# An mLSTM cell feeding a top-1 expert layer: two tiles per expert taken from a count frozen at chunk 18 and run during the routing of the last tiles

## The chip, the cores and the metric

One Trainium2 chip, one of its cores. The metric is the device time of one execution in microseconds; lower is better. Engines are named as in the profile: PE is TensorE (PEld its weight loads), DVE VectorE, ACT ScalarE, POOL GpSimd, SP SyncE.

## What is computed

`q, k, v, o_gate` are (4, 8, 768, 40) in float32, the gates (4, 8, 768). The first part is a recurrence over 768 steps for each batch and head, the second a layer of eight experts on the 3072 rows that come out of it:

```python
for t in range(S):
    m_new = np.maximum(f_gate[:, :, t] + m, i_gate[:, :, t])
    f_stab, i_stab = np.exp(f_gate[:, :, t] + m - m_new), np.exp(i_gate[:, :, t] - m_new)
    C = f_stab * C + i_stab * einsum('bhd,bhe->bhde', vt, kt)
    n = f_stab * n + i_stab * kt
    y[:, :, t] = sigmoid(o_gate[:, :, t]) * (C @ qt) / max(|n . qt|, 1)
x = y.transpose(0, 2, 1, 3).reshape(3072, 320)
logits = x @ w_gate                      # (3072, 8)
expert_idx = logits.argmax(1); gate_w = softmax(logits)[expert_idx]
out = gate_w * (relu(x @ w1[expert_idx]) @ w2[expert_idx])   # 320 -> 1024 -> 320
```

(Shapes are shortened.) With the inputs used, the experts get 508, 638, 184, 320, 431, 317, 284 and 390 rows.

## The kernel before

**The recurrence** is done in 24 chunks of 128 rows (six per batch), in the parallel form: scores of the chunk's rows against each other, plus a state `C` carried from chunk to chunk. The order on every engine is written out by hand: iteration `s` of the loop (from -3) computes the scores of chunk s+1, transposes q and k of s+2, updates the state of s, finishes chunk s (`attend`, `rows`), and routes older chunks. SP issues the loads (L229), six chunks ahead, k, q, v and the output gate each by itself. `rows` (L319 to L325) gives the row tile `x_sb`; `xtrans` (L332) transposes it for the gate logits (L354).

**The routing** goes by pairs of tiles (`teams`), the last two tiles one by one. `choose` takes the best expert of each row, `rank` counts by matmuls with a triangular and a ones matrix how many rows of each expert came before, `place` turns that into a slot. Each expert owns a region of 3200 rows of the DRAM tensor `x_sorted`; `keep_rows` scales a tile by its gate value into `x_all`, and `send` (L447) scatters it from POOL by an indirect DMA. `clear` (L453) zeroes the first 384 rows of each region; ACT issues these eight DMAs during iterations 0 to 3. POOL also issues all loads of the expert weights, since they are cast from float32 to bfloat16 on the way (L167 for w1, in three parts, L171 for w2); experts 0 and 1 are loaded at iterations 17 to 21. `warm` (L434) runs matmuls whose result is not used ("junk"), up to thirty after the last send.

**The experts.** After the last send has landed, SP reads three tiles per expert (384 rows, L593) back into `x_all`. Then groups run in order: experts 0 to 7 with three tiles each, and then six "extra" tiles of experts with more than 384 rows (five are needed here; if more than six were, a loop at the end would run them). A group is: transposes of the row tiles (`turn`, L624), layer 1 (L633: 24 matmuls of 384 columns, results `hp`, relu on DVE and ACT by turns into `h_sb`), the transposes of the next group, layer 2 (L646: eight matmuls per tile, result `zp`), a copy `zo` on ACT (L651) and a scatter to the output from POOL (L652). Weights of experts 2 to 4 are issued after the last send, those of expert 5+i at group i. `extras` works out which tiles are left over, `blank` writes a zero tile after each expert's last row, `collect` fetches an extra tile, `fetch` copies the weights of its expert (`wx`).

Of the kernel before, what the change touches and what calls it, by code (L numbers as in the profile page):

```python
# [19 lines left out]
def kernel(  # L20
# [44 lines left out]
    XU = 6  # L65
    XW = 4
# [46 lines left out]
    for name, shape, pattern, base, mult in (  # L113
        ("first_w", [128, E], [[-1, E]], E, 0),
        ("cum0", [128, E], [[NS // 128, E]], 0, 0),
        ("pos", [128, E, NJ], [[NS, E], [1, NJ]], 0, NJ),
        ("thr", [128, E, NX], [[NS, E], [128, NX]], CAP, 0),
        ("eb", [128, E], [[NS, E]], CAP, 0),
        ("kx", [128, NX], [[1, NX]], 0, 0),
        ("rowx", [128, NX], [[128, NX]], 0, 1),  # L120
    ):
        iotas[name] = (
            consts.tile(shape, I32, name=name + "_i"), consts.tile(shape, F32, name=name), pattern, base, mult,
        )
    first_w, cum0, pos, thr, eb, kx, rowx = (iotas[n][1] for n in iotas)
# [4 lines left out]
    tick = consts.tile([1, 1], F32)  # L130

    def late_consts(i):
# [12 lines left out]
        lo, hi_ = ((0, 2), (2, 4), (4, 7))[i - 2] if 2 <= i <= 4 else (0, 0)  # L145
# [15 lines left out]
    tot = rte.tile([128, E], F32)  # L161

# [20 lines left out]

    def router():
        nc.vector.tensor_scalar_mul(wg_sb[:], wg_sb[:], -1.0)
# [6 lines left out]
    with tc.tile_pool(name="ring", bufs=1) as ring_pool, \  # L192
# [6 lines left out]
        kp, qp, v1 = (  # L199
            [ring_pool.tile([128, H, w], F32, name=f"{n}{i}") for i in range(NV)]  # L200
            for n, w in (("kp", DP), ("qp", DP), ("v1_", D1))
        )
# [58 lines left out]
        def scores(s):  # L261
# [3 lines left out]
            sB = ps1.tile([128, PR, 128], F32, name="sB")  # L265
            for j in range(PR):
# [70 lines left out]
        teams = [(t, t + 1) for t in range(0, NT - 2, 2)] + [(NT - 2,), (NT - 1,)]  # L337
# [8 lines left out]

        def logits(P, host):

            r = rt[P] = {"t": teams[P], "n": len(teams[P])}
            lg, fresh = spare(host)  # L350
            r["lg"] = lg[:, : r["n"] * E]
# [78 lines left out]
        def warm(n):  # L430
            j = ps1.tile([128, 512], F32, name="junk", tag="tk")
            kb = st[NT - 1]["kb"]
            for _ in range(n):
                nc.tensor.matmul(  # L434
                    j[:], lhsT=kb[:, 0, :], rhs=kb[:].rearrange("p j t -> p (j t)"), start=True, stop=True,
                )
# [7 lines left out]
        def send(t):  # L444
            if t >= NT - 7:
                nc.gpsimd.memset(tick[:], 0.0)
            apart(nc.gpsimd.indirect_dma_start(  # L447
                out=xs[:, :], out_offset=bass.IndirectOffsetOnAxis(ap=slots[:, t : t + 1], axis=0),
                in_=x_all[:, t, :], in_offset=None,
            ), "rows_in")  # L450

        def clear(e):
            nc.scalar.dma_start(xs[e * NS : e * NS + CAP, :].rearrange("(p j) d -> p (j d)", j=NJ), zrow[:])  # L453
# [17 lines left out]
        for s in range(-3, NT):  # L471
# [10 lines left out]
            if 0 <= s < E // 2:  # L482
                nc.vector.memset(w1_all[:64, DB - 1, 2 * s : 2 * s + 2, :], 0.0)
                clear(2 * s)
                clear(2 * s + 1)
            if not odd and P >= 0:
                gate(P)
            do(states, s)
            do(load, s + 6 if s >= -1 else -1)
            if not odd and P >= 0:  # L490
                rank(P, s - 1)
            if last:
                warm(2)
                attend(s)
            do(xtrans, s - 1)
            do(ogate, s + 2)
            if not last:
                do(attend, s)
            if s == NT - 2:
                warm(3)  # L500
            if not odd and P >= 0:
                place(P)
            do(keep_rows, s - 4)
            do(rows, s)
            if odd and s >= 3:
# [5 lines left out]
            if 17 <= s < 20:  # L511
                weights_in(0, 2, (s - 17,))
            if 20 <= s < 22:
                weights_out(s - 20, 1)
        P = len(teams) - 3
        send(NT - 5)
        xtrans(NT - 1)
        gate(P)
        rank(P, NT - 1)
        place(P)  # L520
        logits(P + 1, NT)
        choose(P + 1)
        count(P + 1)
        logits(P + 2, NT + 1)
# [3 lines left out]
        gate(P + 1)  # L528
        warm(3)
        rank(P + 1, NT, E)  # L530
        place(P + 1)
        keep_rows(NT - 2)
        send(NT - 2)
        choose(P + 2)
        gate(P + 2)
        warm(3)
        rank(P + 2, NT + 1, E)
        place(P + 2)
        keep_rows(NT - 1)
        send(NT - 1)  # L540
        nc.vector.tensor_copy(tot[:], rt[P + 2]["tot"])
        warm(30)

    xg = [x_all[:, e * NJ : (e + 1) * NJ, :] for e in range(E)]
    sm_pool = ctx.enter_context(tc.tile_pool(name="moe_sm", bufs=1))
    s_idx = sm_pool.tile([128, E, NJ], I32)
    inv = sm_pool.tile([128, E, NJ], F32)
# [39 lines left out]
    mps_pool = ctx.enter_context(tc.tile_pool(name="moe_ps", bufs=3, space=PSUM))  # L587

    def ids_of(t):
        return t[:, :, Dm:].bitcast(I32).rearrange("p j o -> p (j o)")  # L590

    def receive(e):
        nc.sync.dma_start(  # L593
            xg[e].rearrange("p j d -> p (j d)"), xs[e * NS : e * NS + CAP, :].rearrange("(p j) d -> p (j d)", j=NJ),
        )

    def targets(e):
        nc.vector.scalar_tensor_tensor(
            s_idx[:, e, :], in0=inv[:, e, :], scalar=float(N), in1=ids_of(xg[e]), op0=ALU.mult, op1=ALU.add,
        )  # L600
# [11 lines left out]
    def aim(g):  # L612
# [4 lines left out]
        g["si"] = lambda j: t[:, 0:1]  # L617

    def turn(g):
        g["xT"] = wk_pool.tile([128, DB, NJ * 128], BF16, name="xgT")  # L620
        for j in range(g["n"]):
            tp = mps_pool.tile([128, DB, 128], BF16, name="tp", bufs=3)
            for db in range(DB):
                nc.tensor.transpose(tp[:, db, :], g["xg"][:, j, wch[db] : wch[db] + 128], ident_b[:])  # L624
            nc.vector.tensor_copy(g["xT"][:, :, j * 128 : (j + 1) * 128], tp[:])

    def layer1(g):
        cols = g["n"] * 128
        g["h"] = wk_pool.tile([128, FB, NJ * 128], BF16, name="h_sb")
        for fb in range(FB):  # L630
            hp = mps_pool.tile([128, NJ * 128], F32, name="hp")
            for db in range(DB):
                nc.tensor.matmul(  # L633
                    hp[:, :cols], lhsT=g["w"][0][:, db, fb * 128 : (fb + 1) * 128],
                    rhs=g["xT"][:, db, :cols], start=(db == 0), stop=(db == DB - 1),
                )
            if fb % 2 == 0:
                nc.vector.tensor_relu(g["h"][:, fb, :cols], hp[:, :cols])  # L638
            else:
                nc.scalar.activation(g["h"][:, fb, :cols], hp[:, :cols], AF.Relu)  # L640

    def layer2(g):
        for j in range(g["n"]):
            zp = mps_pool.tile([128, Dm], F32, name="zp", bufs=2)
            for fb in range(FB):
                nc.tensor.matmul(  # L646
                    zp[:], lhsT=g["h"][:, fb, j * 128 : (j + 1) * 128], rhs=g["w"][1][:, fb, :],
                    start=(fb == 0), stop=(fb == FB - 1),
                )
            zo = wk_pool.tile([128, Dm], F32, name="zo", bufs=8)  # L650
            nc.scalar.copy(zo[:], zp[:])  # L651
            ins = nc.gpsimd.indirect_dma_start(  # L652
                out=out[:, :], out_offset=bass.IndirectOffsetOnAxis(ap=g["si"](j), axis=0),
# [96 lines left out]
```

## Time and profile before

| what | us |
|---|---|
| runs (three) | 231.73, 233.25, 237.22; median 233.25 |
| profiled execution, its own time | 236.67 |
| its span (first to last instruction) | 234.8 |
| PE, PEld, DVE, ACT, POOL busy in it | 209.9, 169.5, 133.5, 122.7, 124.8 |
| last chunk's L319 | starts at 123.59 |
| first layer 1 of an expert | starts at 142.94 |
| last scatter to the output | issued at 229.63 |

The page divides the span into 40 slices of 5.87 us and gives the busy tenths of each engine, the clock that TensorE was granted, and the DMA engines' share; views of the trace give the same for any stretch, the single instructions in order of time, and what each waited for. Idle time that a row had before it stands in brackets with what ended it. TensorE's ends are modelled, so a full digit says that it had work, not that it ran at its peak; how many matmuls a stretch holds, and the granted clock, say more.

### The profile page before, as it was taken

The page shows a single profiled execution, that of the slowest core. Times are in us where ns is not written, and L with a number is a line of the kernel's source. Part 1 is how long each engine was busy: PE and PEld are TensorE (multiplying, and loading weights), DVE is VectorE, ACT ScalarE, POOL GpSimd, SP SyncE. Part 2 cuts the span into 40 slices and gives each one's busy share as a digit, 9 for nine tenths or more (in the row PEclk, how much of TensorE's full clock was granted, in tenths as well). Part 3 has the DMA queues.
Part 4 walks back from the last instruction along what each step waited for, and adds up shares of the span by engine and source line. Part 5 has one row for each costly group of instructions (what it writes and reads, how often), then busy time and mean ns, then how long its engine had stood idle before and what let it go on. Part 6 is the DMA issues. An engine that isn't in the chain of part 4 may idle for free.

```text
span 234.8 us, 5415 instructions
## 1 busy us (share of the span) xinstructions
PE 209.9 (89%) x1870; PEld 169.5 (72%) x1870; DVE 133.5 (57%) x446; ACT 122.7 (52%) x301; POOL 124.8 (53%) x195
## 2 busy tenths in 40 slices
PE   1389799999999999999998977999959999999990
PEld 1279699999999999999987334756627666668770
DVE  7657754445788888888867203873322453334540
ACT  2557445538688988898836101434223444444440
POOL 5045544343766686689986870433454765433331
PEclk9999955556999999999979597999979999999996
DMA  8999999984979999999697399999999999937900
GB/s 136 191 183 233 210 222 224 191 147 84 171 127 189 177 181 190 200 187 174 120 152 128 68 192 291 239 212 218 235 236 255 227 386 379 375 139 274 355 20 0
DMA packets 121723, 46.45 MB, mean 198 GB/s; under 512 B 102425, under 2 KB 114844, under 8 KB 121696
## 3 DMA queue, kind: packets, MB, share of 16 engines
q1 hardware_dynamic: 106272, 27.52, 54.8%
q0 software_dynamic: 13808, 16.40, 35.5%
q10 hardware_dynamic: 1616, 2.19, 2.6%
q8 instruction: 15, 0.25, 0.4%
q14 instruction: 12, 0.10, 0.1%
HBM read 39.38 MB, written 9.53 MB: 208 GB/s over the span
## 4 chain that ended last, share of the span: by engine, by line
PE 63%; DMA 14%; SPq 7%; DVE 6%; ACT 4%; issue 3%; POOL 2%; ACTq 0%; DVEq 0%; POOLq 0%
PE hp L633 14%; PE zp L646 9%; PE hp L354 7%; PE hp L287 7%; SPq L229 7%; DMA out_dram<-zo,s_idx 6%; PE dC L295 5%; PE tk L254 4%; PE xt L332 4%; PE tq L254 3%; PE sA L267 3%; DMA x_all<-x_sorted 3%; DMA qp<-in_q_dram 2%; DMA o_sb<-in_o_gate_dram 2%; PE hp L307 2%
## 5 line engine op out<-in xcount | busy, mean ns | idle before, releaser
L638 DVE TENSOR_SCALAR h_sb<-hp 128x384 bf16<-128x384 f32 (+1 forms) x56 | 24.6, 443 | 45.9 <-PE hp L633 29.6
L640 ACT ACTIVATE h_sb<-hp 128x384 bf16<-128x384 f32 (+1 forms) x56 | 22.2, 399 | 34.0 <-PE hp L633 33.5
L633 PE MATMUL hp<-xgT,w_all 128*128 128x384 bf16 x192 | 36.0, 345 | 3.8 <-ACT h_sb L640 2.5
L652 POOL DMA_INDIRECT out_dram<-zo,s_idx x24 | 24.0, 999 | 21.8 <-ACT zo L651 9.5
L633 PEld LDWEIGHTS <-w_all 128*128 128x128 bf16 x192 | 19.5, 102 | 18.3 <-issue 7.7
L325 POOL TENSOR_TENSOR x_sb<-x_sb,den 128x320 f32<-128x320 f32 x23 | 16.6, 721 | 27.4 <-DVE den L323 27.3
L646 PEld LDWEIGHTS <-h_sb 128*128 128x128 bf16 x240 | 22.9, 98 | 8.0
L651 ACT COPY zo<-zp 128x320 f32<-128x320 f32 x30 | 12.8, 425 | 30.1 <-PE zp L646 23.0
L447 POOL DMA_INDIRECT x_sorted<-x_all,slots x24 | 25.0, 1040 | 5.8 <-issue 3.5
L646 PE MATMUL zp<-w_all,h_sb 128*128 128x320 bf16 x192 | 27.4, 299 | 0.0
L334 ACT COPY xT<-xt 128x384 f32<-128x384 f32 x24 | 11.6, 482 | 22.7 <-PE xt L332 13.7
L287 PE MATMUL hp<-C_sb,qT 104*128 104x82 f32 x160 | 23.0, 292 | 0.0
L287 PEld LDWEIGHTS hp<-C_sb,qT 104*128 104x128 f32 x160 | 22.2, 214 | 0.5 <-DVE den L321 0.3
L254 PE MATMUL tk<-ident,kp 128*104 128x128 f32 x96 | 18.5, 324 | 4.2 <-DMA kp<-in_k_dram 4.2
L295 PE MATMUL dC<-vA,kp 128*104 128x82 f32 x160 | 21.0, 284 | 0.0
L354 PE MATMUL hp<-wg_sb,xT 128*128 128x8 f32 x144 | 20.3, 273 | 0.0
L295 PEld LDWEIGHTS dC<-vA,kp 128*104 128x104 f32 x160 | 19.6, 200 | 0.0
L354 PEld LDWEIGHTS hp<-wg_sb,xT 128*128 128x128 f32 x144 | 19.5, 215 | 0.1
L275 POOL TENSOR_SCALAR_AFFINE_SELECT dB<-dB 128x512 bf16<-128x512 bf16 x24 | 16.0, 667 | 5.2 <-ACT dB L274 5.0
L274 ACT CAST dB<-sB 128x512 bf16<-128x512 f32 x24 | 14.0, 582 | 8.4 <-PE sB L268 8.3
L242 POOL CAST vAb<-vA 128x328 bf16<-128x328 f32 x24 | 11.0, 459 | 13.4 <-DVE vA L240 12.5
L254 PE MATMUL tq<-ident,qp 128*104 128x128 f32 x96 | 17.5, 314 | 0.5 <-DMA qp<-in_q_dram 0.5
(130 smaller groups left out, 419.5 us busy)
## 6 DMA issues: line engine op xcount, KB each, us to landing
w_all<-in_moe_w_dram POOLq DMA_DIRECT2D x8, 640.0 KB, 13.6
wx<-w_all SPq DMA_DIRECT2D x6, 768.0 KB, 6.1
kp<-in_k_dram SPq DMA_DIRECT2D x24, 160.0 KB, 3.7
qp<-in_q_dram SPq DMA_DIRECT2D x24, 160.0 KB, 3.8
v<-in_v_dram SPq DMA_DIRECT2D x24, 160.0 KB, 4.0
o_sb<-in_o_gate_dram SPq DMA_DIRECT2D x24, 160.0 KB, 4.5
wx<-w_all SPq DMA_DIRECT2D x6, 640.0 KB, 9.6
w_all<-in_moe_w_dram POOLq DMA_DIRECT2D x13, 256.0 KB, 13.9
```

The source lines that it names most:

```text
L229: nc.sync.dma_start(d[n][:, :, :D], src[b, :, c * 128 : (c + 1) * 128, :].rearrange("h p d -> p h d"))
L254: nc.tensor.transpose(tp[:, j, :], two(d[n], j), ident[:])
L287: nc.tensor.matmul(hp[:, 2 * j * D1 : (2 * j + 2) * D1], lhsT=d["qT"][:, j, :], rhs=st["C"][:, j].rearrange("p h d -> p (h d)"), start=(j ...
L295: nc.tensor.matmul(st["dC"][:, j], lhsT=two(d["k"], j), rhs=d["vA"][:, 2 * j : 2 * j + 2, :], start=(c == 0 and j == 0), stop=True, skip_g ...
L325: eng.tensor_tensor(x3d, x3d, den[:].unsqueeze(2).to_broadcast([128, H, D]), op=ALU.mult)
L354: nc.tensor.matmul(lg[:, i * E : (i + 1) * E], lhsT=st[t]["xT"][:, db * 128 : (db + 1) * 128], rhs=wg_sb[:, db, :], start=(fresh and i == ...
L447: apart(nc.gpsimd.indirect_dma_start(out=xs[:, :], out_offset=bass.IndirectOffsetOnAxis(ap=slots[:, t : t + 1], axis=0), in_=x_all[:, t, : ...
L633: nc.tensor.matmul(hp[:, :cols], lhsT=g["w"][0][:, db, fb * 128 : (fb + 1) * 128], rhs=g["xT"][:, db, :cols], start=(db == 0), stop=(db == ...
L638: nc.vector.tensor_relu(g["h"][:, fb, :cols], hp[:, :cols])
L640: nc.scalar.activation(g["h"][:, fb, :cols], hp[:, :cols], AF.Relu)
L646: nc.tensor.matmul(zp[:], lhsT=g["h"][:, fb, j * 128 : (j + 1) * 128], rhs=g["w"][1][:, fb, :], start=(fb == 0), stop=(fb == FB - 1),)
L652: ins = nc.gpsimd.indirect_dma_start(out=out[:, :], out_offset=bass.IndirectOffsetOnAxis(ap=g["si"](j), axis=0), in_=zo[:], in_offset=None ...
```

## The change

- The routing's teams are pairs throughout (the last two tiles go together).
- At team 8 (tiles 16 and 17, the first 18 of 24) the counts are frozen by `even_out`: they are read out, and each expert that has fewer than 256 rows gets its count raised to 256, so that later rows lie behind row 256. The first two tiles of every expert (256 rows) are then final.
- `receive` reads them in the last iteration of the loop, waiting only for the sends up to tile 17. The first two experts' first two tiles run between the routing steps of tiles 20 to 23, in the buffers of the recurrence. There are no junk matmuls in the tail any more.
- Afterwards the groups are (2, first two), (0, third tile), (3, first two), (1, third tile), and so on, and then the six extra tiles. Layer 1 fills a whole PSUM bank (512 columns) before each relu.
- Weights: experts 0 and 1 in iterations 20 to 23, expert 2 in the tail, expert e+1 at group (e, first two): w1 before its layer 1, w2 after it.
- `clear` is issued from SP, in iterations -1 to 2; the memsets of the padding of w1 are halved and spread over iterations 0 to 7.
- Before the scores of chunks 1 to 7 stand three matmuls with 512 columns whose result is overwritten, before those of chunks 21 to 23 two.

```diff
@@ receive, turn and layer1 (moved ahead of the loop, tiles by part) @@
+    def receive(e, part):
+        r0, j = e * NS + part * NE * 128, (NE, NJ - NE)[part]
+        ins = nc.sync.dma_start(
+            xg[e][part].rearrange("p j d -> p (j d)"), xs[r0 : r0 + j * 128, :].rearrange("(p j) d -> p (j d)", j=j),
+        )
+        if part == 0:
+            tc.add_to_no_dep_group("early", getattr(ins, "ins", ins))
...
+    def layer1(g, u):
+        n = g["n"]
+        per = 4 // n
...
+        hp = spot("hp", [128, per, n * 128], F32)
+        for i in range(per):
+            fb = u * per + i
+            for db in range(DB):
+                nc.tensor.matmul(
+                    hp[:, i, :], lhsT=g["w"][0][:, db, fb * 128 : (fb + 1) * 128], rhs=g["xT"][:, db, :],
+                    start=(i == 0 and db == 0), stop=(db == DB - 1), skip_group_check=True,
+                )
@@ scores @@
+            for _ in range(3 if 1 <= s < 8 else 2 if s > NT - 4 else 0):
+                nc.tensor.matmul(
+                    sA[:].rearrange("p j t -> p (j t)"), lhsT=ident_b[:],
+                    rhs=st[s - 1]["dA"][:].rearrange("p j t -> p (j t)"), start=True, stop=True,
+                )
@@ even_out (new), send, clear @@
+            nc.tensor.matmul(c, lhsT=ones_b[:], rhs=row, start=False, stop=True, skip_group_check=True)
+            nc.vector.tensor_copy(cnt[:], c)
+            nc.vector.tensor_tensor(short[:], cnt[:].unsqueeze(2).to_broadcast([128, E, NE]), fill[:], op=ALU.is_lt)
+            for j in range(NE):
+                with nc.allow_low_precision("whole numbers up to 256"):
+                    nc.vector.tensor_tensor(row, row, short[:, :, j], op=ALU.add)
+            nc.vector.tensor_tensor(
+                inv[:, :, :NE], posA[:], cnt[:].unsqueeze(2).to_broadcast([128, E, NE]), op=ALU.is_ge,
+            )
...
+            if t > 2 * PE_ + 1:
+                tc.declare_no_dep(getattr(ins, "ins", ins), group="early", reason="later rows lie behind the early tiles")
...
-            nc.scalar.dma_start(xs[e * NS : e * NS + CAP, :].rearrange("(p j) d -> p (j d)", j=NJ), zrow[:])
+            nc.sync.dma_start(xs[e * NS : e * NS + CAP, :].rearrange("(p j) d -> p (j d)", j=NJ), zrow[:])
@@ the loop @@
-                clear(2 * s)
-                clear(2 * s + 1)
...
+            if -1 <= s < 3:
+                clear(2 * s + 2)
+                clear(2 * s + 3)
...
+            if last:
+                for e in range(E):
+                    receive(e, 0)
...
+            if s == 20:
+                weights_in(0, 1, (0, 1))
+            if s == 21:
+                weights_in(0, 1, (2,))
+            if s == 22:
+                weights_out(0, 1)
+            if last:
+                weights_in(1, 1, range(DB))
@@ the tail @@
+        weights_out(1, 1)
         send(NT - 5)
+        gate(P0)
+        rank(P0, NT - 1)
+        place(P0)
...
+        targets(0, 0)
+        turn(first)
         for t in (NT - 4, NT - 3):
             keep_rows(t)
             send(t)
+        for u in range(4):
+            layer1(first, u)
+        xtrans(NT - 1)
+        targets(1, 0)
+        turn(second)
+        layer2(first, 0)
+        logits(P0 + 1, NT)
+        choose(P0 + 1)
+        gate(P0 + 1)
+        layer2(first, 1)
+        layer1(second, 0)
+        rank(P0 + 1, NT, 2 * E)
+        place(P0 + 1)
+        nc.vector.tensor_copy(tot[:], rt[P0 + 1]["tot"])
+        weights_in(2, 1, range(DB))
+        layer1(second, 1)
+        for t in (NT - 2, NT - 1):
+            keep_rows(t)
+            send(t)
+        for u in range(2, 4):
+            layer1(second, u)
+        weights_out(2, 1)
+        layer2(second, 0)
+        layer2(second, 1)
@@ the groups @@
+    for e in range(E):
+        receive(e, 1)
+    order = [(2, 0), (0, 1)]
+    for e in range(3, E):
+        order += [(e, 0), (e - 2, 1)]
+    order += [(E - 2, 1), (E - 1, 1)]
...
+        if g.get("k") == 0 and nw < E:
+            weights_in(nw, 1, range(DB))
+        for u in range(FB * g["n"] // 4):
+            layer1(g, u)
+        if g.get("k") == 0 and nw < E:
+            weights_out(nw, 1)
         if i + 1 < len(groups):
+            ready(groups[i + 1])
+        for j in range(g["n"]):
+            layer2(g, j)
```

`ready` is `targets` (output rows of a group's slots, one DVE operation) and `turn`; `nw` is the group's expert plus one.

## The prediction

> **What bounds the kernel now.** I read the page's slices first, then the granted clock in stretches, then the rows where a stretch changes. The profiled execution took 236.67 us (span 234.8); the median of the runs is 233.25, so 3.4 us less. I work out differences on the profile and apply them to the median.
>
> The slices on the page: busy tenths of TensorE, its granted clock, the DMA engines.
>
> ```profile
> span 234.8 us, 5415 instructions
> PE   1389799999999999999998977999959999999990
> PEclk9999955556999999999979597999979999999996
> DMA  8999999984979999999697399999999999937900
> ```
>
> TensorE is busy nearly everywhere, but at half clock in slices 6 to 9 and again around slices 21 and 22; one digit low (slice 28) is a stop in the expert stage. DMA is nearly full all along. The clock by stretches (columns: length, busy time and count of PE, PEld, DVE, ACT, POOL, granted clock, DMA share, GB/s):
>
> ```profile
> 26.00:30.00 4.00, 2.24 (x29) 1.98 (x29) 3.04 (x8) 2.78 (x6) 2.44 (x7) 0.96 1.06 245
> 30.00:56.00 26.00, 26.00 (x179) 24.94 (x179) 11.87 (x44) 13.86 (x35) 9.59 (x21) 0.50 0.90 174
> 57.00:117.00 60.00, 59.87 (x722) 57.48 (x722) 49.82 (x173) 51.81 (x131) 45.08 (x63) 1.00 0.97 172
> 118.00:122.00 4.00, 4.00 (x31) 3.30 (x31) 3.29 (x13) 1.57 (x7) 3.17 (x5) 0.57 1.19 170
> ```
>
> So the recurrence (chunks 0 to 23) is bound by TensorE, first at 0.50 and then at 1.00. By the row L319, one per chunk, chunk 2 ends at 27.84, chunk 7 at 59.91, chunk 8 at 65.00, chunk 14 at 88.76: 6.41 us per chunk cold, 3.96 warm. The timeline before the drop:
>
> ```profile
> 24.71 1.63 ACTq L453 DMA_DIRECT2D x_sorted<-zrow  x2
> 27.01 0.52 PE L332 MATMUL xt<-ident,x_sb 128*128 128x128 f32 x3 [0.75 <-ACT xT L334]
> 28.73 0.21 PE L267 MATMUL sA<-qb,kb 40*128 40x128 bf16 x1 [1.01 <-ACT qb L256]
> ```
>
> ScalarE spends 1.63 us issuing two clears (L453), its copies come late, TensorE stands 0.75 and 1.01 us for them, and at 30 the clock halves. The routing tail, in the timeline:
>
> ```profile
> 130.31 9.18 PE L434 MATMUL junk<-kb 104*128 104x512 bf16 x30
> ...
> 131.91 0.96 POOL L447 DMA_INDIRECT x_sorted<-x_all,slots  x1 [0.21 <-issue]
> ...
> 135.50 4.00 SPq L593 DMA_DIRECT2D x_all<-x_sorted  x8
> ...
> 141.42 0.68 PE L624 MATMUL tp<-ident_b,x_all 128*128 128x128 bf16 x9 [1.94 <-DMA x_all<-x_sorted]
> ```
>
> I set t = 0 at the last L319 (123.59). Until t+17.8 TensorE does nothing for the experts: the last send goes at t+8.3, lands at 135.2, its rows come back 5.87 us later. From t+17.8 to the span's end are 93.4 us. An expert of three tiles has a period of 7.66 (187.85, 195.51, 203.17), an extra tile 3.07 (210.50, 213.56); eight and six make 79.7. The last zp ends 5.9 before the span's end. So 7.8 are cold matmuls and the stop at 170 to 172.7.
>
> **What the Trainium skill says.** "TensorE: Matmul & The Clock Gate", Part 1: the array runs at half clock until about 3.4 us of activity, and falls back after an idle window. The trace has both clocks, but the drop at 30 follows idle gaps of only 1 us and stays for 26 us of busy matmuls, so being busy is not enough here. The same page, Part 2, has matmuls in program order: a transpose that waits holds all behind it. "DMA: Bandwidth & Descriptors", "Issuing engines are not separate DMA queues": another issuer saves only issue time; the 1.63 us of ScalarE above are such time. Its "Anatomy of one DMA" gives 2.0 us plus bytes/436e3 for GpSimd's transfers: as an estimate 5.0 us for a w1 (1.31 MB of f32). The trace shows more; see below.
>
> **The change, part by part.**
>
> *Front.* Eight clears move from ACT to SP: 8 x about 0.8 us off ScalarE, the two gaps (1.8 us of TensorE) gone. SP gets 8 issues between the loads. Its loads run ahead: chunk 8's o load is issued at 36.36, and warm chunk 6 would need that chunk's k and q at about 39, so I cost the move at nothing with thin cover; if it is gone, loads are the bound at 4.9 us per chunk (issues at 21.79, 26.63, 31.55, 36.36). Three matmuls of 128x512 before the scores of chunks 1 to 7: warm 0.215 each (the junk pair of L434 took 0.43), so 21 x 0.215 = 4.5 us, all on TensorE's path; cold 0.41 each (three in 1.24). If they hold the clock, chunks 3 to 7 cost 5 x 3.96 = 19.8 instead of 32.1: -12.3. Net -7.8. The eight half-size memsets replace four, hidden by idle DVE.
>
> *End of the loop.* 118 to 122 at 0.57: 4 x 0.43 = 1.7 us to win with the matmuls before the last three scores (6 x 0.215 = 1.3); five junk matmuls (1.24 + 0.43 = 1.7) go. -2.1. Front and end: -9.9.
>
> *Tail.* Counting to 18 tiles adds one matmul and five small DVE operations at 0.17 us to one chunk, beside TensorE: nothing. The early receives wait only for send 17, issued at t-0.8 (122.79): +3.3 landing (131.91 to 135.2) +5.9 gives t+8.4. TensorE then has in order: transposes and copy 1.3; 24 matmuls of 256 columns, cold at two thirds of the 0.32 between the cold 384-column ones after 143.2, 5.1 (t+14.8); the transposes of tile 23 and of the second group, 1.0; layer 2 of one tile, 1.1; logits 1.4 (t+18.3); layer 2, 1.1; first unit of the second, 0.7; ranks 0.3; three units 2.0; layer 2, 2.2: t+24.5. The last routing thus stands behind expert work: where sends 22 and 23 went at t+7.1 and t+8.3, POOL now first issues two output scatters (each waits for its zo) and three w1 loads of expert 2, so they go at about t+23.7 and t+25; landed t+29, rows of the third tiles back at t+34 (80 KB, 5.7 for the like xgx). The transposes of (0, third tile) stand ahead of layer 2 of (2, 0), so TensorE stops there about 3 us, and about as long before for expert 2's w1. Third group (3, 0) begins at t+40. Matmuls alone would be there at t+32.7.
>
> *Experts.* Cutting 3 into 2 + 1 costs: 24 x 0.11 (two thirds of 3.90/24) + 0.45 (six of nine transposes in 0.68) + 16 x 0.136 (3.26/24) = 5.3, plus one tile 2.95 (between the 3.07 of an extra and its summed rows): 8.2 against 7.66. What is late next are weights. Before, five experts' weights were issued by 147.7, far ahead; now expert e+1's loads are issued when (e, 0) starts, one pair ahead, after the preceding scatter on POOL (zo 0.65 after layer 2, 0.28, 0.98, 0.3: 2.2 us). How long an expert takes then, in this profile:
>
> ```profile
> 175.81 1.73 POOL L167 DMA_DIRECT2D w_all<-in_moe_w_dram  x3
> 177.46 1.00 POOL L171 DMA_DIRECT2D w_all<-in_moe_w_dram  x1
> ```
>
> Expert 7's w1 landed 9.5 us after the first issue (SP's fetch, which waits for it, goes at 185.63), its w2 12.6 after (188.39), with backlog; expert 2's w1 took 6.6 (132.87 to 139.5) without. So a pair lasts at least 2.2 + 6.6 = 8.8 and at most 11.7; I take 9.3, nearer the low end, since no backlog can build up. Four pairs bring (7, 0) to t+77.2. Then 5.3 + 9 x 2.95 = 31.8 and 5.9 behind: t+115 against t+111.2. **+3.7.** Bounds: pairs at 8.2 and half the tail's stops -4.5; pairs at 11.7 +13.3. The number of extra tiles needed stays within the six that run anyway (rounding up lifts only experts below 256 rows, none above 384), so the loop for more stays shut. wx fetches (6 x 1.4 MB) have from t+86 to t+97 as cover; enough at 6.1 and 9.6 us landing.
>
> Sum: -9.9 + 3.7 = -6.2 on 233.25: **227.0 us**.
>
> **The rivals.**
>
> A, *the clock isn't held*: cold matmuls add 15 x 0.41 + 6 x 0.215 = 7.4 and win nothing but the gaps (1.8): +5.6. With +3.7 for the rest 242.6. For it: the clock stayed low for 26 us with TensorE busy all the time, and fell again at 118 after 60 busy us. Against: dense bf16 matmuls did bring it back in the junk run (thirty in 9.18 us: the first 3.4 us cold at 0.41, the others warm at 0.215 would take 8.1). It decides as soon as fewer than about two of the five cold chunks are warmed. It is the slower case.
>
> B, *weights become the bound of the expert stage* at expert 7's 11.7 a pair: +9.6 more, 236.6; POOL's issues held by scatters make it likelier, the lighter DMA load less.
>
> C, *the tail overlaps better* and pairs run at TensorE's 8.2: -4.5 instead of +3.7, 218.9. Against it: the transposes in order, POOL in order.
>
> D, *loads take the front's gain*: 4.9 instead of 4.6 (3.96 + 0.65) and the gaps that follow halve it: 231.
>
> **How the numbers follow.** Main case (222 to 230) 0.36, A 0.25, B 0.18, C 0.11, D 0.10. A measurement tells about 2% (4.7 us) from nothing, so faster is below 228.6 and slower above 237.9. Faster: 0.36 x 0.95 + C = 0.45. Slower: A 0.24 and 0.07 from B with colder matmuls after its stops = 0.31. The rest, 0.24, is within. The range leaves out the better half of C and the worst of A with B together: 217 to 244. The likeliest case's own range is 222 to 230.
>
> **What would show it.** Clock 1.00 from 20 to 60 and L319 of chunk 7 near 49 with the last near 114 (front right); 0.50 there is A. In the tail the first expert transposes 8 us after the last L319, sends 22 and 23 some 24 us after, a stop of TensorE before the transposes of the first third tile. Between layer-1 starts of successive pairs 8.8 to 9.8 us, ended by w_all DMAs; 8.2 without such waits is C, above 11 is B. Wrong in principle I would be if the span fell while the front stayed at 6.4 us per chunk, or if another engine than TensorE or a weight load ended the pairs.

## The result, and the profile after

The changed kernel takes 247.95 us (median of four runs, 245.43 to 249.96) where the kernel before, run beside it, takes 235.24: ratio 1.058, 95% interval 1.040 to 1.075. It is slower; 227.0 had been predicted. Ratios and intervals, here and below, are of the fast runs alone (those within 1.5% of their kernel's fastest), while times are medians of all runs. The profiled execution took 245.43 us, the shortest of its four, and that of the kernel before 236.67, above its median; so the two profiles are only 8.9 us apart where the medians are 12.7. The page of the changed kernel, span and slices:

```profile
span 243.7 us, 5754 instructions
PE   1399996759999999999970895767788888989991
PEclk9999999985599999999995699599999999999997
DMA  9999999999999999999359989997999999999950
```

Counted from 1, the clock is full through slice 8, as hoped, and falls in slices 9 to 11. But TensorE has holes in slices 7 to 9 that weren't there before. The timeline of TensorE names what ended them (start, length, line, operation, and in brackets the idle time before it and what ended it):

```profile
39.26 0.62 PE L340 MATMUL tk<-ident,kq 128*104 128x128 f32 x4 [1.63 <-DMA kq<-in_k_dram]
45.08 0.62 PE L340 MATMUL tk<-ident,kq 128*104 128x128 f32 x4 [0.49 <-DMA kq<-in_k_dram]
51.58 0.62 PE L340 MATMUL tk<-ident,kq 128*104 128x128 f32 x4 [3.09 <-DMA kq<-in_k_dram]
```

TensorE waits for k: the front has become bound by loads. By the start of L410 (the row L319 of before), which stands for a chunk's end here and in all that follows, chunk 7 ends at 56.0 (59.9 before), chunk 8 at 65.0 in both, chunk 19 at 108.99 against 107.44, the last one at 126.05 against 123.59. So the front gained nothing by chunk 8. Another 1.6 us were lost up to chunk 19 (1.2 of them in chunk 9, where the clock was still halved until 67.0) and 0.9 behind it: +2.5 us, where -9.9 was predicted.

The loads are slow from the very start, long before a clear or an extra matmul is there. Stretches of the kernel before (last two columns: DMA share, GB/s):

```profile
3.00:10.00 7.00, 2.13 (x8) 1.34 (x8) 6.50 (x19) 2.82 (x4) 1.13 (x3) 1.00 1.27 199
10.00:18.00 8.00, 6.16 (x44) 5.22 (x44) 3.97 (x9) 5.24 (x10) 3.14 (x9) 1.00 1.06 183
```

The same of the changed kernel:

```profile
3.00:10.00 7.00, 2.13 (x8) 1.34 (x8) 6.50 (x19) 2.82 (x4) 1.13 (x3) 1.00 1.47 152
10.00:18.00 8.00, 6.84 (x54) 5.47 (x55) 4.07 (x9) 5.64 (x11) 3.15 (x9) 1.00 1.49 155
```

The queues are busier (1.49 against 1.06) and carry less (155 against 183 GB/s): each packet takes longer. The packets of 160 bytes (one head's row of k, q, v or o, which the profile records one by one) take 23.0 ns on average in the first 12 us and 24.9 in the next 12; before, 16.0 and 14.8.

The tail went nearly as worked out. With t = 126.05:

```profile
134.26 0.82 PE L232 MATMUL tp<-ident_b,x_all 128*128 128x128 bf16 x6 [5.31 <-DMA x_all<-x_sorted]
...
151.05 0.28 PE L244 MATMUL hp<-xT,w_all 128*128 128x256 bf16 x1 [1.50 <-DMA w_all<-in_moe_w_dram]
...
154.08 4.88 PE L244 MATMUL hp<-xT,w_all 128*128 128x256 bf16 x22 [1.34 <-DMA w_all<-in_moe_w_dram]
...
160.89 0.34 PE L232 MATMUL tp<-ident_b,x_all 128*128 128x128 bf16 x3 [1.94 <-DMA x_all<-x_sorted]
```

First transposes at t+8.2, stops for expert 2's w1, a stop before the first third tile; (3, 0) begins at t+41.0. From there pairs last 10.96, 9.13, 10.15 and 9.57 us (layer-1 starts 167.09, 178.05, 187.18, 197.33, 206.90; (3, 0) is expert 3's first two tiles, and a pair is such a group with the single third tile behind it). From t to the span's end are 117.6 us, 111.2 before: +6.4 against +3.7.

### The profile page after: what moved, and what is told of

The parts are those of the page before. It is cut to its first block, busy times and chain, and to the rows that moved or that the text cites. A ratio compares the mean times of both kernels' runs of the same rounds, so it can differ in the third digit from the quotient of the medians.

```text
span 243.7 us, 5754 instructions
## 1 busy us (share of the span) xinstructions
PE 199.5 (82%) x2049; PEld 167.4 (69%) x2049; DVE 130.3 (53%) x421; ACT 119.4 (49%) x275; POOL 127.4 (52%) x202
## 3 DMA queue, kind: packets, MB, share of 16 engines
q0 software_dynamic: 13856, 16.40, 36.6%
## 4 chain that ended last, share of the span: by engine, by line
PE 35%; DMA 17%; issue 14%; DVE 14%; POOL 10%; ACT 5%; SPq 4%; POOLq 1%; DVEq 0%; ACTq 0%
POOL out_dram L264 6%; DMA x_all<-x_sorted 5%; PE hp L378 5%; DMA w_all<-in_moe_w_dram 4%; PE dC L386 4%; PE hp L446 4%; PE tk L340 4%; PE zp L257 3%; DMA x_sorted<-x_all,slots 3%; PE tq L340 3%; PE hp L244 3%; PE xt L423 2%; DMA kq<-in_k_dram 2%; DMA kq<-in_q_dram 2%; PE sA L358 2%
## 5 line engine op out<-in xcount | busy, mean ns | idle before, releaser
L250 DVE TENSOR_SCALAR h<-hp 128x512 bf16<-128x512 f32 x26 | 17.9, 690 | 44.0 <-PE hp L244 38.7
L244 PEld LDWEIGHTS <-w_all 128*128 128x128 bf16 x384 | 31.7, 102 | 11.0 <-DMA w_all<-in_moe_w_dram 5.0
L244 PE MATMUL hp<-xT,w_all 128*128 128x128 bf16 (+1 forms) x336 | 31.8, 252 | 4.1 <-DMA w_all<-in_moe_w_dram 4.1
L252 ACT ACTIVATE h<-hp 128x512 bf16<-128x512 f32 x26 | 15.5, 597 | 37.4 <-PE hp L244 25.0
L257 PE MATMUL zp<-w_all,h 128*128 128x320 bf16 x160 | 25.2, 300 | 8.4 <-ACT h L252 5.0
L257 PEld LDWEIGHTS <-h 128*128 128x128 bf16 x208 | 17.8, 98 | 19.9 <-ACT h L252 8.2
L545 POOL DMA_INDIRECT x_sorted<-x_all,slots x24 | 25.1, 1047 | 10.2 <-DMA kq<-in_k_dram 6.0
L340 PE MATMUL tk<-ident,kq 128*104 128x128 f32 x96 | 17.2, 307 | 9.6 <-DMA kq<-in_k_dram 5.2
L262 ACT COPY zo<-zp 128x320 f32<-128x320 f32 x26 | 11.1, 426 | 25.0 <-PE zp L257 22.2
L378 PE MATMUL hp<-C_sb,qT 104*128 104x82 f32 x160 | 21.7, 280 | 0.2 <-DVE sm L515 0.2
L326 DVE TENSOR_TENSOR vA<-v,G_T 128x328 f32<-128x328 f32 x24 | 16.6, 692 | 7.0 <-DMA v<-in_v_dram 6.4
L328 POOL CAST vAb<-vA 128x328 bf16<-128x328 f32 x24 | 11.1, 460 | 16.4 <-DVE vA L326 15.9
L386 PE MATMUL dC<-vA,kq 128*104 128x82 f32 x160 | 19.2, 267 | 0.0
L340 PEld LDWEIGHTS tk<-ident,kq 128*104 128x104 f32 x96 | 10.6, 140 | 12.4 <-issue 5.6
L425 ACT COPY xT<-xt 128x384 f32<-128x384 f32 x24 | 11.6, 482 | 14.8 <-PE xt L423 12.6
L386 PEld LDWEIGHTS dC<-vA,kq 128*104 128x104 f32 x160 | 17.7, 184 | 0.0
```

The lines of the kernel that those rows point to most:

```text
L244: nc.tensor.matmul(hp[:, i, :], lhsT=g["w"][0][:, db, fb * 128 : (fb + 1) * 128], rhs=g["xT"][:, db, :], start=(i == 0 and db == 0), stop= ...
L250: nc.vector.tensor_relu(dst, hp)
L252: nc.scalar.activation(dst, hp, AF.Relu)
L257: nc.tensor.matmul(zp, lhsT=g["h"][:, fb, j * 128 : (j + 1) * 128], rhs=g["w"][1][:, fb, :], start=(fb == 0), stop=(fb == FB - 1),)
L326: nc.vector.tensor_tensor(d["vA"][:], d["v"][:], Gb.unsqueeze(2).to_broadcast([128, H, D1]), op=ALU.mult)
L340: nc.tensor.transpose(tp[:, j, :], two(d[n], j), ident[:])
```

## Experiments

"Last L410" also stands for L319 in copies of the kernel before. The kernel before ran beside every group, on several chips; its own medians there lie between 232.8 and 242.3, so a time is read beside the one given with it. Where a ratio has no interval beside it, none is on record.

### Why are the loads slow? Five runs against four suspects

```diff
# b_pad: kernel before; a_pad: changed kernel
+    shift = rte.tile([128, 8], F32)
# a_clr: changed kernel
-            nc.sync.dma_start(xs[e * NS : ...
+            nc.scalar.dma_start(xs[e * NS : ...      (issued in chunks 0 to 3)
# a_sep: changed kernel
-        kq = ring_pool.tile([128, NV, 2, H, DP], F32)
+        kq = ring_pool.tile([128, 2, NV, H, DP], F32)
# b_kq: kernel before, with the changed kernel's three lines for kq, kp and qp
```

> The kernel before with one unused tile of 32 bytes a partition put ahead of the k and q tiles, so that their addresses, multiples of 64 plus 32 until now, become multiples of 64 (as in the changed kernel), and those of o the reverse. Theory 'addresses': the loads' writes are slower at the changed kernel's addresses; between 3 and 10 us they move about 150 GB/s instead of 199, and the time is 1.01 to 1.03 of the kernel before. Theory 'clears on SP' (the clears among the loads make them late) and theory 'the chip of the day': no difference, ratio 1.00 within 0.015, about 200 GB/s as in the kernel before.

> The changed kernel with the same unused 32 bytes, which put the addresses of k, q, v and o back to the kernel before's remainders. Theory 'addresses': about 200 GB/s between 3 and 10 us instead of 152, chunk 8 ends near 57 instead of 65, the last L410 near 118 instead of 126, time 239 to 241. Theory 'clears on SP': no change, 152 GB/s, TensorE still waits for k at 39 and 51, 247 to 249.

> The changed kernel with the eight clears put back on ScalarE at the kernel before's place, chunks 0 to 3. Theory 'clears on SP': the waits for k at 39 and 51 are gone, chunk 8 ends near 57, the last L410 near 118 to 120, time 240 to 242. Theory 'addresses': loads still move 152 GB/s between 3 and 10 us, waits for k remain at least half as long, and ScalarE's gaps of 0.75 and 1.01 us come back: 246 to 250.

> The changed kernel, its one tile of k and q laid out as all k and then all q (12,288 bytes a partition from a chunk's k to its q, as in the kernel before) instead of k and q by turns (2,048 bytes). Theory 'interleaved tile': the packets of 160 bytes take 15 to 16 ns on average in the first 24 us, as in the kernel before (23 to 25 in the changed kernel), loads move about 195 GB/s between 3 and 18 us instead of 154, TensorE's waits for k at 39 and 51 go, chunk 8 ends near 57, time 240 to 242. Theory 'something else in the program': 23 to 25 ns, no change of time.

> The kernel before with the changed kernel's one interleaved tile for k and q and nothing else. Theory 'interleaved tile': packets of 160 bytes take 23 to 25 ns in the first 24 us, loads move 155 GB/s, the front becomes bound by loads and the ratio is 1.01 to 1.03. Theory 'something else in the program': 15 to 16 ns and a ratio of 1.00 within 0.015.

Packets of 160 bytes between 12 and 24 us, mean:

| kernel | k starts at byte (of 256) | ns | time, us | before beside it |
|---|---|---|---|---|
| before | 32 | 14.8 | | |
| b_pad | 64 | 14.7 | 235.7 | 232.8 |
| b_kq | 32 | 15.5 | 238.8 (ratio 1.024, 1.012 to 1.036) | 237.3 |
| after | 192 | 24.9 | 247.95 | 235.2 |
| a_pad | 224 | 25.8 | 247.7 | 232.8 |
| a_clr | 192 | 25.2 | 248.8 | 232.8 |
| a_sep | 192 | 25.3 | 247.25 (1.055, 1.040 to 1.070) | 237.3 |

A shift of 32 bytes, the clears on SP, the interleaving and the chip all leave the packets as they were. Copies of the kernel before are fast, copies of the changed kernel slow. b_kq's time is above what its fast loads explain, but not in the loop: its last L319 comes at 118.6, 5 us earlier than in the page of before. It loses 9 us behind it, where TensorE stands 5.4 and 3.3 us for ScalarE (one stop of 2.5 in the page of before); the longer of these begins with ScalarE waiting for a scatter to the output. Why, no run tells. What does go with the speed is the second column. It is worked out from where the tiles lie in a partition of SBUF: k and q have rows of 160 bytes at a pitch of 256, so all of them start at the same byte of a 256-byte block, and behind 96 each crosses into the next block. The new tiles (`cnt`, `short`, `inv`, `s_idx` and others) had pushed the ring 416 bytes up, from 32 to 192.

### Rows that cross a 256-byte block

```diff
+    shift = rte.tile([128, 16], F32)    # a_al: changed kernel, k at byte 0;  b_96: kernel before, 96
+    shift = rte.tile([128, 24], F32)    # b_128: kernel before, 128
+    shift = rte.tile([128, 40], F32)    # b_un and b_kqo: kernel before, 192
+        shift2 = ring_pool.tile([128, 24], F32)    # b_kqo too, between q and v
```

> The changed kernel with an unused tile of 64 bytes a partition ahead of the ring, so that a row of k or q (160 bytes, one per head at a pitch of 256) starts at byte 0 of a 256-byte block instead of byte 192. In the kernel before it starts at byte 32 (in the padded copy at 64), and no row crosses a 256-byte boundary; in the changed kernel and its copies run so far it starts at 192 or 224, and every row crosses one. Theory 'crossing rows': packets of 160 bytes take 15 to 17 ns in the first 24 us instead of 23 to 25, loads move about 195 GB/s instead of 154, TensorE doesn't wait for k before chunk 8, chunk 8 ends near 57, the last L410 near 119 to 121, time 239 to 243. Theory 'something else in the program': 23 to 25 ns, chunk 8 at 61 to 65, 246 to 249.

> The kernel before with an unused tile of 160 bytes ahead of the ring, so that its rows of k and q start at byte 192 of a 256-byte block instead of 32 and cross a boundary. Theory 'crossing rows': packets of 160 bytes take 23 to 25 ns in the first 24 us, loads move about 155 GB/s between 3 and 18 us, TensorE waits for k in chunks 4 to 8 where the clock is full, ratio 1.01 to 1.03. Theory 'something else in the program': 15 to 16 ns, 195 GB/s, ratio 1.00 within 0.015.

> The kernel before with an unused tile of 64 bytes ahead of the ring: rows of k and q start at byte 96 of a 256-byte block and end just at its end (96 + 160 = 256). Theory 'crossing rows': as the kernel before, packets of 160 bytes 15 to 16 ns on average between 12 and 24 us. If only the distance from byte 32 matters: in between, 18 to 22 ns.

> The same with 96 unused bytes: rows of k and q start at byte 128 and cross the boundary by 32 bytes. Theory 'crossing rows': 23 to 26 ns between 12 and 24 us, a sudden step from the run before with only 32 bytes between them. If the start has to be at 192 or behind: 15 to 16 ns.

> The kernel before with 160 unused bytes ahead of k and q and 96 behind them: k and q start at byte 192, while v and o stay at the bytes of their blocks that they have in the kernel before. If k's and q's rows are the cause: packets of 160 bytes 23 to 26 ns between 12 and 24 us. If it is v's or o's: 15 to 16 ns. If all share it: 18 to 21.

| kernel | k at byte | ns, 12 to 24 us | last L410 | time, us | before beside it |
|---|---|---|---|---|---|
| a_al | 0 | 14.6 | 118.8 | 241.4 (1.020, 1.012 to 1.028) | 235.7 |
| b_un | 192 | 25.0 | 133.8 | 252.8 (1.067, 1.059 to 1.075) | 235.7 |
| b_96 | 96 | 15.0 | 114.9 | 228.3 (one run) | 236.4 |
| b_128 | 128 | 23.9 | 133.0 | 248.8 (one run) | 236.4 |
| b_kqo | 192, v and o as before | 23.3 | 132.8 | 248.45 (one run) | 236.4 |

The step lies between byte 96, where a row just ends with its block, and 128. The loads' queue in the first 20 us (packets, MB, share of 16 engines' time), of b_96:

```profile
q1 hardware_dynamic: 20581, 3.24, 99.1%
```

and of b_128, which differs by 32 unused bytes:

```profile
q1 hardware_dynamic: 16762, 2.64, 119.3%
```

0.991 x 16 x 20 us over 20,581 packets are 15.4 ns each; 1.193 x 320 us over 16,762 are 22.8. Fewer rows come in, and each costs more. b_kqo shows that moving k and q alone does it. Not told apart from the crossing is a start in the upper half of a block: every slow case starts at 128 or behind, every fast one at 96 or before. Rows of another length could tell; none was run. o's rows lie at a pitch of 160 bytes and half of them cross a block in the kernel before too, at no price that shows; why, no run tells. The packet times of "crossing rows" held in all five runs. In a_al chunk 8 came at 57.4, as written down, though chunk 7 came as early as 49.6: a stretch of halved clock from 50.6 on lay between. b_un lost more than the 1.01 to 1.03 written down. Its last L319 came at 133.8, 10 us later than in the page of before, and another 6 us were lost behind the loop, where no k or q is loaded; of these the cause is open.

### Do the extra matmuls hold the clock?

```diff
# b_dum: kernel before, ahead of the scores
+            for _ in range(3 if 1 <= s < 8 else 0):
+                nc.tensor.matmul(sA..., lhsT=ident_b[:], rhs=st[s - 1]["dA"]..., start=True, stop=True)
```

> The kernel before with the three extra 128x512 matmuls ahead of the scores of chunks 1 to 7 and nothing else of the change. If they hold the clock and loads keep up (the prediction's front): clock near 1.00 from 30 to 60, chunk 7 ends near 53 instead of 59.9, ratio 0.97. If loads are the bound all the same (the prediction's rival D): clock near 1.00 but waits for k or q from chunk 5 on, ratio 0.985 to 1.00. If the clock is not held (rival A): 0.50 from 30 to 56 and ratio 1.02.

The median is 235.4 against 232.8 for the kernel before, the fastest run 226.8 against 226.2. In the profiled run the clock was 1.00 until 106, and chunk 7 ended at 51.1; then a cold stretch (the clock at half) of 13.7 us came, and the last L319 was at 121.5. That looks like the prediction's front, but b_pad, which has no extra matmul, was cold for only 3.4 us at 30, ended chunk 7 at 50.2, and had its 17.1 cold us at 105. The cold stretch of the kernel before isn't tied to chunks 3 to 7: it comes early or late. (a_best and a_best0 below try the same in the changed kernel.)

### The expert stage

```diff
# a_lag: layer 2 behind the next group's layer 1
-        for j in range(g["n"]):
-            layer2(g, j)
+        for g_ in groups[i - 1 : i] if i else []:
+            for j in range(g_["n"]):
+                layer2(g_, j)
# a_w: weights two experts ahead
+    weights(3, 1)
-        nw = g.get("e", E) + 1
+        nw = g.get("e", E) + 2
# a_lagw: both
```

> The changed kernel, in the expert loop layer 2 of each group moved behind layer 1 and the transposes of the next. Theory 'exposed relu' (each pair loses 0.7 to 1.0 us in the middle of layer 2 of its single tile, where TensorE waits for ScalarE's relu): these stops go, pairs last 8.2 to 8.8 where no weights are late, 9.0 where they are; from the first pair to the end about 4 us less, 243 to 244. Theory 'weights' (the prediction's price for pairs): the stops move to layer 1 of the pair, which now comes earlier and waits for w_all; pairs stay at 9.3 to 10, no gain.

> As the run before, and each expert's weights asked for one pair earlier (two experts ahead). Theory 'exposed relu': little more than that run brings, up to 1 us. Theory 'weights': pairs fall to TensorE's own 7.7 to 8.2 us only here, 241 to 243. If both share the loss: pairs near 8.2 here and near 9 in that run.

> The changed kernel with weights asked for two experts ahead and layer 2 left where it is (the fourth corner to the changed kernel, layer 2 moved, and both). From the last L410 to the end it is 117.5 us in the changed kernel, 116.8 with layer 2 moved, 111.1 with both. Theory 'two bounds side by side' (exposed relu and late weights each hold pairs near 9.5): 115 to 117 and pairs of 9.0 to 9.4 here, the exposed relu left. Theory 'weights alone': 111 to 112.5 and pairs of 8.2 or less. Time 241 to 247.

a_lag and a_lagw also fetch the weights of the last two extra tiles behind layer 2. Pairs are read between the layer-1 starts of (3, 0) to (7, 0). The first five rows have the same expert stage, with layer 2 and weights as in the changed kernel. "Relu" is TensorE's time in stops named after a relu of ScalarE within the four pairs, "weights" that in stops named after `w_all`:

| kernel | the four pairs, us | sum | relu | weights | last L410 to the end | time, us | before beside it |
|---|---|---|---|---|---|---|---|
| after | 11.0, 9.1, 10.2, 9.6 | 39.8 | 3.3 | 1.4 | 117.6 | 247.95 | 235.2 |
| a_sep | 11.1, 9.0, 10.5, 9.4 | 40.0 | 4.1 | 1.3 | 120.8 | 247.25 | 237.3 |
| a_al | 11.2, 9.2, 10.5, 9.2 | 40.1 | 3.7 | 1.5 | 121.1 | 241.4 | 235.7 |
| a_pad | 10.1, 8.4, 9.9, 9.1 | 37.5 | 0 | 3.2 | 117.1 | 247.7 | 232.8 |
| a_clr | 10.1, 7.9, 11.9, 8.5 | 38.3 | 0 | 4.2 | 117.3 | 248.8 | 232.8 |
| a_lag | 8.7, 10.5, 9.1, 9.0 | 37.3 | 0 | 4.2 | 116.9 | 247.9 | 237.3 |
| a_w | 10.1, 7.8, 7.8, 7.8 | 33.4 | 0 | 0 | 112.8 | 239.7 | 236.4 |
| a_lagw | 8.5, 7.7, 8.0, 8.8 | 33.0 | 0 | 0 | 111.3 | 240.7 (1.023, 1.002 to 1.044) | 237.3 |

In the changed kernel, a single tile (its 24 matmuls of layer 1, the next group's transposes, the two halves of layer 2) reads:

```profile
183.25 1.50 PE L244 MATMUL hp<-xT,w_all 128*128 128x128 bf16 x24
184.59 0.50 PE L232 MATMUL tp<-ident_b,x_all 128*128 128x128 bf16 x6
184.93 0.72 PE L257 MATMUL zp<-w_all,h 128*128 128x320 bf16 x4
185.97 0.60 ACT L252 ACTIVATE h<-hp 128x512 bf16<-128x512 f32 x1 [2.09 <-PE tp L232]
186.62 0.72 PE L257 MATMUL zp<-w_all,h 128*128 128x320 bf16 x4 [0.98 <-ACT h L252]
```

ScalarE's relu begins 1.2 us after the matmuls it needs (183.25 + 1.50), and TensorE stands 0.98 us for it. In a_w, with the same order of work:

```profile
190.52 1.50 PE L244 MATMUL hp<-xT,w_all 128*128 128x128 bf16 x24
191.86 0.50 PE L232 MATMUL tp<-ident_b,x_all 128*128 128x128 bf16 x6
192.11 0.60 ACT L252 ACTIVATE h<-hp 128x512 bf16<-128x512 f32 x1 [0.96 <-PE hp L244]
192.19 1.28 PE L257 MATMUL zp<-w_all,h 128*128 128x320 bf16 x8
```

the relu begins at once and no stop follows. By its numbers a_w went as "weights alone" had it. But the relu that is in time there isn't the doing of earlier weights, for it is in time in a_pad too, whose weights are asked for one pair ahead:

```profile
182.06 1.50 PE L244 MATMUL hp<-xT,w_all 128*128 128x128 bf16 x24
183.65 0.60 ACT L252 ACTIVATE h<-hp 128x512 bf16<-128x512 f32 x1 [0.96 <-PE hp L244]
183.74 1.28 PE L257 MATMUL zp<-w_all,h 128*128 128x320 bf16 x8
...
189.79 2.33 PE L257 MATMUL zp<-w_all,h 128*128 128x320 bf16 x16 [1.12 <-DMA w_all<-in_moe_w_dram]
```

So there are two losses side by side. Where the relu is in time, weights one pair ahead give sums of 37.5 and 38.3, with stops named after the weights; a_lag, which hides the relu, gives the same 37.3; two experts ahead it is 33.4. Where the relu is late, some 2 us come on top (39.8 to 40.1). What makes it late isn't known. The addresses alone don't, for a_clr has the changed kernel's; nor does the chip alone, for a_sep ran on that of a_pad and a_clr. In the late cases the trace names the transposes behind layer 1 as what released the relu, and the ends of TensorE's instructions are modelled, so the matmuls may have ended later than they are shown. That was not tried; a_all below, where no such stop comes back in the pairs, speaks against it. The first pair holds another, smaller one: a stop of 1.7 to 1.9 us for VectorE's relu behind the operations of `extras`, in all runs but those with layer 2 moved. What a_lag gains over the changed kernel, 2.5 us, is mostly lost again at its end, where the last two extra tiles wait 0.7 and 1.7 us for their weights, which there can be fetched only when a buffer is free.

One profile of each kernel is a weak witness for the whole stretch to the end. In the copies of the kernel before, which are the same behind the loop, it lasts from 110.9 us (b_pad) to 120.4 (b_kq). The stops inside the pairs are what these readings rest on.

### Addresses and weights put right, and a better kernel

```diff
# a_fix: changed kernel + shift of 64 bytes + weights two ahead (a_w)
# a_all: a_fix + layer 2 behind the next layer 1 (a_lag)
# a_best: a_all, and
-        weights_in(2, 1, range(DB))            (expert 2's weights now after send 21)
-    order = [(2, 0), (0, 1)]
+    order = [(2, 0), (3, 0), (0, 1)]           (and so on)
# a_best0: a_best without the extra matmuls of chunks 1 to 7
-            for _ in range(3 if 1 <= s < 8 else 2 if s > NT - 4 else 0):
+            for _ in range(2 if s > NT - 4 else 0):
```

> The changed kernel with the 64 bytes, layer 2 moved behind the next group's layer 1, weights two experts ahead with those of expert 2 asked for after send 21 (before the first layer 1), and expert 3's first two tiles put ahead of expert 0's third. If rows that cross and late weights are what it lost: the last L410 at 119 to 121, the first layer 1 of expert 2 without a stop, no wait for the rows of the third tiles (7 us between the second and third group before), from the last L410 to the end 103 to 106 instead of 117.5, time 224 to 230, ratio 0.95 to 0.98. If the weights asked for early delay the sends and the receives instead: 108 to 112 from the last L410, ratio 0.99 to 1.01.

> As the run before without the three extra matmuls ahead of the scores of chunks 1 to 7. If they hold the clock (the prediction): a cold stretch of 10 us or more begins by 30 to 40 and the time is 4 to 8 us above that of the run with them. If they do not, but only cost their 4.5 us, the cold stretches add up to the same within 7 us and the time is the same or up to 4 us below.

> The changed kernel with the two suspects taken out and nothing else: 64 unused bytes ahead of the ring (rows of k and q start at byte 0 of a 256-byte block) and weights asked for two experts ahead. If these two are the whole loss against the prediction: packets of 160 bytes 15 ns, chunk 8 near 57, the last L410 at 116 to 120, 112 to 113 us from there, 228 to 233 us, ratio 0.97 to 0.99 (the prediction was 227.0, 0.973). If a third loss is left: ratio 1.00 to 1.02.

> The run before this one plus layer 2 moved behind the next group's layer 1, so that a relu that starts 1.1 us late no longer stands in front of TensorE. If the stops named after ScalarE's relu (0.7 to 1.0 us, one or two a pair, in the changed kernel and in that run) are the third loss: from the last L410 to the end 110 to 112 us instead of 118.3, pairs of 7.6 to 8.5, ratio 0.96 to 0.98. If something delays TensorE itself and the relu is only where it shows: stops come back in front of layer 1 or the transposes, 115 to 118, ratio 0.985 to 1.00.

| kernel | last L410 | to the end | time, us | before beside it |
|---|---|---|---|---|
| a_fix | 117.8 | 118.5 | 240.9 | 242.3 |
| a_all | 115.4 | 114.1 | 231.3 (0.968, 0.960 to 0.976) | 235.0 |
| a_best | 115.4 | 113.5 | 230.9 (0.972, 0.963 to 0.981) | 235.7 |
| a_best0 | 118.5 | 110.8 | 229.7 (0.964, 0.957 to 0.971) | 235.7 |

a_fix's front is what was expected, its tail is not: its four pairs sum to 36.6 us, not to a_w's 33.4, with relus again 0.8 to 1.3 us late and stops of 0.73 to 1.01 us named after them. Its ratio to the kernel beside it, 0.994 by the medians and 0.983 by the fastest run of each, doesn't decide between two losses (0.97 to 0.99 had been written down) and three (1.00 to 1.02); the late relu in the trace is what speaks for the third. a_all hides the relu: the four pairs are 7.9, 7.7, 8.0 and 7.9 with 0.2 us of stops in them, and the stretch to the end is 4.4 us shorter, though one stop of 2.5 us, named after VectorE's relu, keeps it from the 110 to 112 expected. It beats the kernel before, and with its ratio of 0.968 the changed kernel (1.058) too. a_fix and a_w have the same order of work and differ by 64 unused bytes and the chip; why the relu is late in one and not in the other was not found.

a_best and a_best0 are as fast as a_all, not faster: the 103 to 106 from the last L410 was not reached. In a_best0 TensorE no longer waits for the third tiles' rows, but 3.0 us for expert 3's w1 (three stops, 148 to 151) and up to 2.4 for VectorE's copies. And the extra matmuls bring nothing that can be measured (230.9 with, 229.7 without). Without them a cold stretch of 10.2 us came at 49, with them none did in the profiled run before 117, and still the times are the same; whether they hold the clock and cost as much as they save, or do neither, one profile of each can't tell.

## Why the prediction was wrong

- **Front, -7.8.** Measured at chunk 8: 0.0 (64.98 against 65.00), with 5.2 us of stops for k before it. The step that failed is "I cost the move at nothing with thin cover": loads were taken at the old kernel's pace. The moved clears did cost nothing (a_clr). What took the cover away is a part of the change that the sum has no term for: the new tiles ahead of the ring, which moved k and q from byte 32 to 192. Rival D had the mechanism (loads take the front's gain), for another reason and with too small a price. With the shift undone (a_al), chunk 7 ends at 49.6, where "near 49" had been said.
- **The clock, -12.3 + 4.5.** The second thing wrong in that term. I took one profile's cold stretch, 27 us from 30 on, for a property of those chunks. A copy with the same instructions in the loop (b_pad) had 3.4 us there, and 17.1 at 105. The matmuls put in against it changed no time measurably (b_dum, a_best against a_best0), so neither the main case nor rival A describes it. Where a_al's chunk 7 comes as early as forecast, it isn't shown that they brought it there.
- **End of the loop, -2.1.** From chunk 19 to 23 the changed kernel needs 17.06 us, the kernel before 16.15: +0.9, although its clock was at 1.00 and the kernel before was cold for 3.4 us of it. Chunk 20, where the counts are rounded up, takes 6.45 instead of 5.17. The small operations costed at nothing stand before its L410 on VectorE, some 0.8 us of them:

```profile
114.66 0.17 DVE L527 COPY cnt<-hp 128x8 f32<-128x8 f32 x1
114.86 0.18 DVE L528 TENSOR_TENSOR short<-cnt,fill 128x16 f32<-128x16 f32 x1
115.08 0.37 DVE L531 TENSOR_TENSOR cums<-cums,short 128x8 bf16<-128x8 bf16 x2
115.36 0.17 DVE L532 TENSOR_TENSOR inv<-posA,cnt 128x16 f32<-128x16 f32 x1
115.44 0.48 DVE L410 SCALAR_TENSOR_TENSOR x_sb<-th,hp 128x320 f32<-128x320 f32 x1
```

From there to chunk 23 the changed kernel needs 10.6 us, the kernel before 11.0 with its cold stretch, so only 0.4 of it came back. How much of the rest reaches TensorE was not tried.
- **Tail.** Right within 2 us, and at its end within 1: t+8.2 (8.4), sends 22 and 23 at t+21.7 and t+23.1 (23.7, 25), (3, 0) at t+41.0 (40).
- **Experts, +3.7.** Measured +6.4: the tail gave 1.0 more than forecast, the four pairs 2.6 more (39.8 us instead of 37.2, so that (7, 0) starts at t+80.9 instead of t+77.2), the rest 0.9 less. The term mis-sized is the pair, taken at 9.3. Its mechanism, weights asked for one pair ahead, is there: where the relu is in time, such pairs sum to 37.5 and 38.3 (a_pad, a_clr), and with weights two experts ahead they take 7.8 (a_w), so that TensorE's own 8.2 was too high. But in the measured run every pair ended with a stop named after ScalarE's relu (3.3 us in all), not after the weights (1.4). The prediction had called another engine at a pair's end a sign of being wrong in principle, and for that part it was: a late relu, costed at nothing, is in neither the sum nor the rivals. Why it is late stays open.

Together, in the profiles: +2.5 and +6.4 instead of -9.9 and +3.7. With the three losses taken out (a_all) the ratio is 0.968; predicted was 227.0 / 233.25 = 0.973. That these agree is in part luck. a_all has another order of layer 2 and of weights than the kernel that was predicted, its pairs take 7.9 instead of 9.3, and the clock term of -12.3, the largest of the sum, was not shown to exist. One reading of the page was off as well, without weight in the sum: the low digit of TensorE stands in slice 30, not 28.

## What to carry to other kernels

Where a change allocates anything, compare the addresses of the tiles that strided DMAs write. Here all rows of k and q came to cross a 256-byte block at once, and the sign was packets that took longer from the first microseconds on (23.0 ns instead of 16.0). Don't bank on the place of a cold stretch from one profile; ask several. And when a run removes a stop, look whether the stop is also missing in runs that don't have the edit: a_w alone would have laid the late relu on the weights.

## What the hardware showed beyond that

- With k's and q's rows of 160 bytes starting at byte 128, 192 or 224 of a 256-byte block, the mean packet of 160 bytes took 23 to 26 ns between 12 and 24 us; at 0, 32, 64 or 96 it took 15 to 16. The kernel before with 160 unused bytes (b_un) was 6.7% slower, not all of it in the loop.
- Cold stretches came in multiples of 3.41 us (3.4, 6.8, 10.2, 13.7, 17.1, 20.5, 27.3, 30.7), but for those that the end of the span cuts off. The Trainium skill, "TensorE: Matmul & The Clock Gate", Part 1, names a window of 3,413 ns on which the clock is decided; the traces agree with that, but not with its account that one busy window brings the full clock back: in the kernel before TensorE was busy for 26.00 of the 26.00 us from 30 to 56 with the clock at 0.50.
- b_128 was cold for 27.3 us at 26 and for 27.3 at 118, b_96 for 3.4 at 44 and 6.8 at 119: so slow loads may cost a second time through the clock. One profile of each is not enough to say so.
